# A top-k attention and SwiGLU kernel: one more block by halves, and a different FFN share in the early units

## The chip, the cores and the metric

The kernel runs on one core of one Trainium2 chip. The core has five engines that work side by side, each through its own list of instructions in order: TensorE (matmul, "PE" in the profile; its weight loads are listed apart as "PEld"), VectorE ("DVE"), ScalarE ("ACT"), GpSimd ("POOL") and SyncE ("SP", which issues most DMAs here). The metric is the device time of one execution in microseconds. Lower is better.

## The reference, cut to what matters

The inputs are q, k and v of shape (8, 8, 576, 64): 8 batches, 8 heads, 576 positions, head size 64. Three weight matrices follow for the feed-forward network (FFN).

```python
scores = scale * np.matmul(q, k.transpose(0, 1, 3, 2))
kth = np.partition(scores, -top_k, axis=-1)[..., -top_k:-top_k + 1]     # top_k = 32
scores = np.where(scores >= kth, scores, -1000000000.0)
scores = scores - np.max(scores, axis=-1, keepdims=True)
attn = np.exp(scores)
attn = attn / (np.sum(attn, axis=-1, keepdims=True) + 1e-09)
x = np.matmul(attn, v)                 # then transposed and reshaped to (4608, 512)
g = x @ w_gate                         # 512 -> 1536
silu = g * (1.0 / (1.0 + np.exp(-g)))
out = (silu * (x @ w_val)) @ w_out     # 1536 -> 512
```

All is float32.

## The kernel before, in words

**Units.** Attention is cut into 160 units. A unit is a pair of heads of one batch and a tile of 128 query rows. A batch has 20 units: four full query tiles (576 = 4 x 128 + 64) of four head pairs each, and four units for the last 64 rows. These last units handle one 128-row tile of two half-height heads, so they cost VectorE about half ("short" units below; units 16 to 19, 36 to 39, 56 to 59 and so on). `AHEAD` is 8 * NHP = 32, where NHP = 4 is the number of head pairs.

**What a unit does.** `scores` (lines 288 to 331) multiplies q and k on TensorE and ScalarE copies the result to SBUF as `sc`. `select` (333) finds the 32 largest scores of each row on VectorE: four rounds of MAX8, with a MATCH_REPLACE8 between rounds that writes into the tile `e`. `weigh` (367) turns scores into exponentials on ScalarE, `normalize` (387) divides by their sum (reciprocal on VectorE, one head's multiply on ScalarE and the other's on GpSimd). `turn` (403) transposes the weights on TensorE into a PSUM tile `etps`, and ScalarE copies them to `et`. `values` (423) multiplies by v on TensorE, and ScalarE copies the result into `xT` (465), the input of the FFN. `prep` (257) transposes q and k of a head pair once per batch.

**The FFN.** The 4608 tokens form 18 blocks of 256. For each block, gate and value products (line 604, 256 columns wide) are followed by ScalarE and GpSimd work for the SwiGLU, and then by an output product built from seven quarters (line 670). The first `HALVED` blocks take their gate and value products in two halves of 128 tokens each (`feed_half`, line 502, products in line 517), so that the first half can start before the second half's tokens exist. The first block also has a plain output product (line 569), since the output weights are only combined for the seven quarters later.

**The order of the work.** The main loop (line 870) writes the instructions of all engines unit by unit. In unit n TensorE gets the scores of units ahead, the values of units n-4 and n-3 (even n only), the transposes of unit n-2, prep of a unit ahead, and in between pieces of the FFN. `piece` (777) issues one small piece and returns its cost: 1 for a gate or value step, 0.75 for half a quarter, 0 where no work is ready because tokens are missing. How many pieces a unit gets is set by `share` (813): an allowance of `beside` for a full unit (half of it for a short one) minus a cost for the attention work of that unit, and not less than `least`. What a unit does not use is kept as `credit`, but never more than one piece above the next share. The last four units and the end take all that is left.

Every engine keeps the written order (lines 940 to 953), so a wait of one instruction holds all that follows on its engine. The pools that matter here: `sc` and `e` have three buffers, the PSUM pool `ps_t` (scores, values, transposes, prep) has five, `ps_f` (FFN) three.

Of the kernel before, what the change touches and what calls it, by code (L numbers as in the profile page):

```python
# [25 lines left out]
def kernel(  # L26
# [43 lines left out]
    NHP = H // 2  # L70
# [2 lines left out]
    MS = MC // 2  # L73
    MQ = MC // 2
    NBLK = B * S // BLK
    HALVED = 3
    AHEAD = 8 * NHP
    scale = 1.0 / float(D) ** 0.5
    assert D == 64 and R == 64 and H * D == DM and DM == 512 and B * S % BLK == 0
# [204 lines left out]
    def n_heads(qt):  # L284

        return 1 if qt == J else 2
# [203 lines left out]

    halves_of = {(kb, t): [] for kb in range(HALVED) for t in range(2)}
    fed, told = [], []

    def tokens(kb, t):

        ends = [0]
        for b in range(B):
            ends += [b * S + min(S, (qt + 1) * P) for qt in range(J + 1)]
        end = min(x for x in ends if x >= kb * BLK + (t + 1) * P)
        return NHP * min(end - kb * BLK, BLK)  # L500
# [86 lines left out]
    def feed(kb):  # L587
# [3 lines left out]

        if kb in range(2, HALVED):
            for t in range(2):
# [27 lines left out]
        def pair(m, t):  # L621

            if kb < HALVED:
                return halves_of[kb, t][m // 4][:, m % 4 : m % 4 + 2, :]
# [4 lines left out]

        for s in range(MS if kb >= HALVED else 0):  # L630
            h = ffn.tile([P, 2, BLK], FP32, tag="h", name="h", bufs=MS + 1)
# [145 lines left out]
    def piece():  # L777
# [13 lines left out]
        while True:  # L791
            if not current:
                if not todo or done.get(todo[0], 0) < tokens(todo[0], int(todo[0] >= HALVED)):
                    return 0
# [18 lines left out]
    def share(n):  # L813


        others = 0.0
        for m, cost in [(m, 0.7) for m in valued(n)] + [(n - TURN, 0.6)]:
            if m >= 0:
                others += cost * (0.5 if units[m][1] == J else 1)
        others += 0.7 * len(scored(n))  # L820
        if units[n + 3][1] == 0:
            others += 0.6

        beside = 5.8 if n < AHEAD else 6.25
        least = 2.0 if n >= 3 * NHP and n % 2 == 0 else 0.0
        return max(least, beside * n_heads(units[n][1]) / 2 - others)

    def scored(n):

        ahead = [n + 1] if n < 2 else [] if n % 2 else [n + 1, n + 2]  # L830
        return [m for m in ahead if m < NU and (units[m][1] < J or m % 2 == 0)]

    def valued(n):

        behind = [] if n % 2 else [n - 4, n - 3]
        return [m for m in behind if 0 <= m < NU]
# [33 lines left out]
    for n in range(NU + 3):  # L870
# [16 lines left out]
        if n >= NU - NHP:  # L887
            credit[0] = 8.0
        else:
            credit[0] = min(credit[0] + share(n), share(n) + 1)  # L890
# [93 lines left out]
```

## Time and profile before

| what | us |
|---|---|
| median of 3 runs | 1713.33 |
| lowest, highest | 1712.2, 1714.15 |
| profiled execution | 1712.03 |
| its span in the profile | 1710.2 |
| TensorE busy | 1647.4 (96%) |
| VectorE busy | 1476.5 (86%) |
| ScalarE busy | 1259.5 (74%) |
| GpSimd busy | 799.0 (47%) |

The page cuts the span into 40 slices of 42.8 us, and each digit is the busy share in tenths. "PEclk" is the clock that the throttle granted to TensorE. In a group or a timeline, a line has the start and duration or the busy time, the engine, the line of the kernel, the operation, what is written and read, and the number of instructions; "<-" behind an idle time names what ended it. A float32 matmul shows as two rows in the trace, so one gate or value product of 256 columns is two rows.

### The profile page before, as it was taken

The page shows a single profiled execution, that of the slowest core. Times are in us where ns is not written, and L with a number is a line of the kernel's source. Part 1 is how long each engine was busy: PE and PEld are TensorE (multiplying, and loading weights), DVE is VectorE, ACT ScalarE, POOL GpSimd, SP SyncE. Part 2 cuts the span into 40 slices and gives each one's busy share as a digit, 9 for nine tenths or more (in the row PEclk, how much of TensorE's full clock was granted, in tenths as well). Part 3 has the DMA queues.
Part 4 walks back from the last instruction along what each step waited for, and adds up shares of the span by engine and source line. Part 5 has one row for each costly group of instructions (what it writes and reads, how often), then busy time and mean ns, then how long its engine had stood idle before and what let it go on. Part 6 is the DMA issues. An engine that isn't in the chain of part 4 may idle for free.

```text
span 1710.2 us, 32128 instructions
## 1 busy us (share of the span) xinstructions
PE 1647.4 (96%) x11600; PEld 1398.2 (82%) x11600; DVE 1476.5 (86%) x3311; ACT 1259.5 (74%) x2901; POOL 799.0 (47%) x914
## 2 busy tenths in 40 slices
PE   5588999999999999999999999999999999999999
PEld 3477698987888887888888888888888888888887
DVE  7999899998989899997999989998999979999400
ACT  7899887877767787768676887777777778676531
POOL 4798545352444425353535334444344433535434
PEclk6699999999999999999999999999999999999999
DMA  7533120003000030001200030000400011000000
GB/s 210 139 112 99 29 72 2 14 1 79 22 13 1 15 86 14 1 8 42 51 14 1 13 74 27 2 13 2 98 1 13 2 44 29 13 2 13 1 13 13
DMA packets 109310, 59.74 MB, mean 35 GB/s; under 512 B 88544, under 2 KB 96992, under 8 KB 109152
## 3 DMA queue, kind: packets, MB, share of 16 engines
q1 hardware_dynamic: 108016, 57.37, 12.9%
q8 instruction: 91, 1.49, 0.4%
q14 instruction: 67, 0.55, 0.1%
q10 hardware_dynamic: 1136, 0.33, 0.1%
HBM read 48.23 MB, written 9.44 MB: 34 GB/s over the span
## 4 chain that ended last, share of the span: by engine, by line
PE 88%; DVE 5%; ACT 4%; DMA 1%; POOL 1%; issue 1%; SPq 0%; POOLq 0%; ACTq 0%
PE f L604 37%; PE x_ps L670 10%; PE av L448 9%; PE s L325 8%; PE y_ps L670 8%; PE etps L412 7%; PE f L517 6%; DVE m L347 2%; DVE e L351 2%; PE kqps L271 1%; PE o_ps L569 1%; PE s L308 1%; ACT e L379 1%; DVE size L124 1%; ACT e L374 0%
## 5 line engine op out<-in xcount | busy, mean ns | idle before, releaser
L347 DVE MAX8 m<-e 128x8 f32<-128x576 f32 x864 | 617.9, 755 | 3.3
L351 DVE MATCH_REPLACE8 e<-m,e 128x576 f32<-128x576 f32 x576 | 425.4, 748 | 0.0
L604 PE MATMUL f<-xT,wg 128*128 128x256 f32 x1440 | 335.9, 382 | 1.3 <-ACT xT L465 1.3
L604 PE MATMUL f<-xT,wv 128*128 128x256 f32 x1440 | 331.4, 380 | 0.0
L604 PEld LDWEIGHTS f<-xT,wg 128*128 128x128 f32 x1440 | 268.9, 190 | 49.0 <-issue 13.1
L604 PEld LDWEIGHTS f<-xT,wv 128*128 128x128 f32 x1440 | 268.2, 190 | 37.5 <-issue 3.8
L640 POOL TENSOR_TENSOR h<-h,half_g 128x512 f32<-128x512 f32 x90 | 114.7, 1275 | 349.2 <-ACT h L639 349.2
L330 ACT ACTIVATE sc<-s 128x288 f32<-128x288 f32 x512 | 170.4, 431 | 105.2 <-PE s L325 104.6
L413 ACT COPY et<-etps 128x512 f32<-128x512 f32 (+1 forms) x448 | 183.6, 486 | 66.0 <-PE etps L412 65.6
L379 ACT ACTIVATE e<-e,bias 128x576 f32<-128x576 f32 x288 | 221.7, 780 | 12.7 <-POOL bias L362 9.7
L374 ACT ACTIVATE e<-sc,m 128x576 f32<-128x576 f32 x288 | 212.3, 792 | 0.6 <-DVE m L347 0.5
L351 DVE MATCH_REPLACE8 e<-m,sc 128x576 f32<-128x576 f32 x288 | 212.6, 748 | 0.0
L412 PE MATMUL etps<-ident,e 128*128 128x128 f32 x1312 | 178.2, 280 | 33.7 <-POOL e L399 15.0
L347 DVE MAX8 m<-sc 128x8 f32<-128x576 f32 x288 | 204.0, 747 | 7.5 <-ACT sc L330 7.5
L412 PEld LDWEIGHTS etps<-ident,e 128*128 128x128 f32 x1312 | 156.2, 144 | 54.7 <-POOL e L399 19.2
L645 POOL TENSOR_TENSOR h<-h,val 128x512 f32<-128x512 f32 x90 | 114.8, 1275 | 155.0 <-ACT val L644 152.4
L325 PE MATMUL s<-kqT 64*128 64x288 f32 x1024 | 169.2, 441 | 13.7 <-ACT sc L330 7.5
L399 POOL TENSOR_TENSOR e<-e,tot 128x576 f32<-128x576 f32 x140 | 161.1, 1154 | 28.5 <-DVE tot L393 28.2
L448 PE MATMUL av<-et,v 128*64 128x128 f32 (+1 forms) x2560 | 158.0, 268 | 0.0
L448 PEld LDWEIGHTS av<-et,v 128*64 128x64 f32 x2560 | 137.7, 140 | 5.9 <-ACT kqT L268 2.7
L325 PEld LDWEIGHTS s<-kqT 64*128 64x128 f32 x1024 | 94.2, 190 | 58.3 <-issue 18.4
L397 ACT ACTIVATE e<-e,tot 128x576 f32<-128x576 f32 x148 | 119.1, 805 | 21.7 <-DVE tot L393 21.6
(86 smaller groups left out, 2249.1 us busy)
## 6 DMA issues: line engine op xcount, KB each, us to landing
v<-in_v_dram SPq DMA_DIRECT2D x32, 256.0 KB, 3.3
kq_in<-in_k_dram SPq DMA_DIRECT2D x63, 128.0 KB, 2.8
kq_in<-in_q_dram SPq DMA_DIRECT2D x63, 128.0 KB, 2.9
w<-in_moe_w_gate_dram SPq DMA_DIRECT2D x12, 512.0 KB, 3.8
w<-in_moe_w_val_dram SPq DMA_DIRECT2D x12, 512.0 KB, 3.8
w<-in_moe_w_out_dram SPq DMA_DIRECT2D x12, 512.0 KB, 3.5
out_dram<-o SPq DMA_DIRECT2D x38, 128.0 KB, 2.4
out_dram<-o SPq DMA_DIRECT2D x16, 256.0 KB, 2.5
```

The costliest lines, as they stand in the source:

```text
L325: nc.tensor.matmul(ps[:, 0:half], slab[d, q0 : q0 + P], slab[d, k0 : k0 + half])
L330: nc.scalar.mul(sc[:, i * half : (i + 1) * half], ps[:, 0:half], scale)
L347: nc.vector.max(m[:, t, 8 * r : 8 * r + 8], cur[:, hs])
L351: nc.vector.match_replace(e[:, hs], m[:, t, 8 * r : 8 * r + 8], cur[:, from_[t]], LOWEST)
L374: nc.scalar.activation(e[:, hs], sc[:, at], AF.Prelu, bias=m[:, t, TOP_K - 1 : TOP_K], scale=-1.0, alpha=SMALL,)
L379: nc.scalar.activation(e[:, hs], e[:, hs], AF.Exp, bias=bias[:, t : t + 1], scale=-1.0 / SMALL, accum_out=tot[:, t : t + 1],)
L399: nc.gpsimd.tensor_tensor(e[:, hs], e[:, hs], tot[:, t : t + 1].to_broadcast([P, S]), ALU.mult)
L412: nc.tensor.transpose(ps[:, c * P : (c + 1) * P], e[:, k0 : k0 + P], ident[:])
L413: nc.scalar.copy(et[:, c0 : c0 + cn, :], ps[:, 0 : cn * P].rearrange("p (c j) -> p c j", c=cn),)
L448: nc.tensor.matmul(av[d, i, 0:ql], weights_, moving, start=c == (0 if last else J), stop=c == (J if last else J - 1),)
L604: nc.tensor.matmul(ps[:, i, :], w[:, kc, m * P : (m + 1) * P], x[:, kc, :], start=(kc == 0), stop=(kc == KC - 1),)
L670: nc.tensor.matmul(ps, lhsT, T[i][m], start=m == 0, stop=m == MQ - 1)
```

## The change

Three numbers are changed. `HALVED` goes from 3 to 4, so that block 3, the fourth, takes its gate and value products in halves of 128 tokens, as the first three do. `beside` is 5.2 in place of 5.8 for units 16 to 27 (the 17th to the 28th). `least`, the two pieces that every even unit got at the least from unit 12 on, now applies from unit 32 on.

```diff
-    HALVED = 3
+    HALVED = 4
...
-        beside = 5.8 if n < AHEAD else 6.25
-        least = 2.0 if n >= 3 * NHP and n % 2 == 0 else 0.0
+        beside = 5.2 if 4 * NHP <= n < 7 * NHP else 5.8 if n < AHEAD else 6.25
+        least = 2.0 if n >= AHEAD and n % 2 == 0 else 0.0
         return max(least, beside * n_heads(units[n][1]) / 2 - others)
```

## The prediction

> **What bounds the kernel now.** I read the page's busy shares and slices first, then the chain, then stretches cut at unit borders, then single waits. A unit begins where VectorE runs its first MAX8 on that unit's scores. Units are numbered from 0 as in the code, so "the 33rd unit" is unit 32.
>
> ```profile
> PE 1647.4 (96%) x11600; PEld 1398.2 (82%) x11600; DVE 1476.5 (86%) x3311; ACT 1259.5 (74%) x2901; POOL 799.0 (47%) x914
> ...
> PE   5588999999999999999999999999999999999999
> ...
> PEclk6699999999999999999999999999999999999999
> ...
> PE 88%; DVE 5%; ACT 4%; DMA 1%; POOL 1%; issue 1%; SPq 0%; POOLq 0%; ACTq 0%
> ```
>
> TensorE is short of work only in the first four slices (170 us); after that it carries the end. A microsecond is won after that only by removing a TensorE wait or TensorE work. The stretches show where waits are left: units 16 to 27, 28 to 35, 36 to 37, 38 to 64, 65 to 66.
>
> ```profile
> 193.32:302.76 109.44, 108.04 (x947) 94.37 (x946) 99.76 (x214) 85.38 (x207) 50.41 (x59) 1.00 0.15 37
> 302.76:386.74 83.98, 83.95 (x741) 76.27 (x741) 78.79 (x176) 64.80 (x151) 37.07 (x45) 1.00 0.02 8
> 386.74:400.03 13.29, 11.14 (x128) 9.07 (x128) 11.31 (x26) 10.98 (x28) 5.20 (x7) 1.00 0.25 57
> 400.03:665.15 265.12, 265.12 (x1833) 224.71 (x1830) 243.12 (x555) 199.38 (x465) 111.77 (x136) 1.00 0.13 32
> 665.15:685.06 19.91, 17.59 (x124) 14.39 (x123) 19.84 (x47) 16.75 (x39) 5.79 (x7) 1.00 0.07 27
> ```
>
> After each span come TensorE, weight loads, VectorE, ScalarE and GpSimd, then the granted clock. TensorE is full in 28 to 35 and 38 to 64 and idle 1.4, 2.1 and 2.3 us in the other three. In units 16 to 27 VectorE, not TensorE, has the slack: 9.7 us. What it waits for there (total, times, longest):
>
> ```profile
> DVE e L351 <- PE etps L412: 8.3, 4, 2.7
> ```
>
> A MATCH_REPLACE8 may not overwrite the tile e until the transposes three units back have read it. TensorE has been given too much there and reaches them late.
>
> Units 36, 37 and 65 are dry. Following the plan's credit through the code, these units issue no FFN piece: block 2's output is finished, and block 3 (or 5) waits for tokens. TensorE runs up to VectorE and stands:
>
> ```profile
> 392.76 1.27 PE L412 MATMUL etps<-ident,e 128*128 128x128 f32 x9 [0.38 <-ACT xT L465]
> 395.77 1.20 PE L412 MATMUL etps<-ident,e 128*128 128x128 f32 x9 [1.75 <-ACT e L397]
> ```
> ```profile
> 670.92 0.92 PE L325 MATMUL s<-kqT 64*128 64x288 f32 x4 [0.99 <-ACT et L413]
> ...
> 677.73 2.64 PE L604 MATMUL f<-xT,wg 128*128 128x256 f32 x11 [1.32 <-ACT xT L465]
> ```
>
> Busy time hides part of a wait, as ends of matmuls are modelled. I count from start to start against the usual pace of the same rows (40 rows of av 2.33 us, 8 of s 1.17, 9 of etps 0.98). From 386 to 400 us the excess is 0.3 + 0.45 + 2.1 + 0.2 = **3.0 us**, from 665 to 680 us 1.4 + 1.7 = **3.1 us**. In units 16 to 27 it is 2.7 us (0.58 at 206.81, 0.76 at 222.22, 0.65 at 223.13, 0.57 at 297.29, 0.16 at 277.33).
>
> **The change, part by part.** The order of instructions gives FFN pieces per unit, in the plan's own cost (a piece is 1; half an output quarter, 6 rows of 216 ns or 1.30 us, is 0.75):
> - units 16 to 19: 2, 2, 2, 2 before; 0, 2, 0, 1 after
> - units 20 to 27: 3, 5, 3, 6, 1.75, 5.25, 2.25, 5.25; after 3, 5, 2, 5, 1, 5, 2, 4.5
> - units 28 to 35: 31.5 in all; after 32.25
> - units 36 to 39: 0, 0, 3, 2; after 1.5, 2.25, 2.25, 2.25
> - units 40 to 64: 98.5 before, 98.25 after
> - unit 65: 0; after 5.25. From unit 66 on both orders are the same.
>
> So nothing is moved beyond about 685 us; the end moves by what TensorE does and waits up to there.
>
> *Block 3 by halves.* 192 rows of 256 columns become 384 rows of 128.
>
> ```profile
> 355.39 3.74 PE L517 MATMUL f<-xT,wg 128*128 128x128 f32 x32
> 358.96 1.95 PE L517 MATMUL f<-xT,wv 128*128 128x128 f32 x16
> ...
> 406.17 1.89 PE L604 MATMUL f<-xT,wv 128*128 128x256 f32 x8
> 407.90 0.60 PE L271 MATMUL kqps<-ident,kq_in 128*128 128x128 f32 x4
> ```
>
> By starts, 32 half rows take 3.57 us and 8 full rows 1.73, so two half pieces take 3.57 against 3.46: 0.11 x 12 = **+1.3 us**. The other engines do the same: six gates and six values of 128x512 either way. The early start of a half brings nothing, as block 3 begins only in unit 40, where both halves' tokens are there. From below the edit is 0 (if a weight load covers it), from above 2.8 us, by busy time (71.4 + 70.6 us for 1152 half rows, 667.3 us for 2880 full ones); I take the paces, nearest to a full TensorE.
>
> *Smaller share and no least share, units 16 to 27.* 9 leave in the plan's cost: 3 pieces at 1.79 us and 8 half quarters at 1.30, 15.8 us of TensorE work. VectorE gives back at most the 8.3 us of that row, so TensorE must either use up its lag behind VectorE (2.9 us at unit 28: 305.66 against 302.76) and run ahead, or wait. I walked both engines by the rows above. From 194.34 us unit 16's values and scores and the transposes of unit 14 end near 198.9, in time for e, so the 2.7 us wait in unit 17 goes and unit 18 begins at 204.9 instead of 207.5. Now TensorE, with no piece to run, is late next for three things: in unit 18 the transposes need the bank that the xT copy frees, about 209.1 against 207.9 (1.1 us); in unit 19 they need ScalarE's multiply, queued behind three copies of prep (0.9 us); in unit 20 scores need the bank of the etps copy, queued behind weigh (1.2 + 0.7 us). Units 20 to 27 have 6.9 pieces a pair on the mean: 6.6 us of attention (8 + 8 rows of s, 40 of av, 18 of etps) and 12.2 of FFN against VectorE's two 9.69. A lag of 2 us that prep leaves at unit 21 carries them to unit 28, where the xT copy is late by 0.9. In all about 5.0 us of waits in place of 2.7: **+2.3 us**. Queued behind those transposes are prep and the scores of the unit after next, but VectorE has its scores a unit ahead, so it does not stop. Ends: from below -2.7, if no wait stays; from above +4.5, if of the 15.8 us only the 8.3 come back and no lag is used (7.2 us of waits). I take the walk, between them.
>
> *Refilled units.* In 36 and 37 two and three half quarters stand where TensorE waited, and lag is 2 us at unit 36, so ScalarE's multiply is there first: **-3.0 us**. In 65 seven half quarters (9.1 us) run; unit 66's xT copy then comes during the first two row groups: **-3.1 us**. Ends for each: nothing won (the lag is lower than I think and the same wait comes back) and the whole.
>
> SP: the first output's store moves behind two sets of key and query loads. A load follows the prep two units earlier, some 10 us ahead of its use; four issues took 4.1 us (207.87 to 211.9) and landing takes 2.8 (page, median). GpSimd is idle 54% of units 16 to 27. Both at nothing; with that cover gone a prep comes up to 3 us late.
>
> **Sum:** 1.3 + 2.3 - 3.0 - 3.1 = **-2.5 us** on a profiled execution of 1712.03 us (span 1710.2, 1.8 around it). The median of the runs is 1.3 above that execution: 1713.33 - 2.5 = **1710.8 us**. A measurement of this kernel tells about 0.2% (3.4 us) from no change, and -2.5 is inside.
>
> The row for the clock: TensorE stood from 106.9 to 110.83 us, and then:
>
> ```profile
> 111.16:114.57 3.41, 3.41 (x18) 0.50 0.00 0
> 114.57:118.00 3.43, 1.16 (x11) 1.00 0.68 191
> 118.00:121.40 3.40, 3.18 (x16) 0.50 0.31 120
> ...
> 81.00:88.00 7.00, 4.48 (x39) 1.00 0.30 76
> ```
>
> A wait of 3.8 us was followed by 3.4 us at half clock, and so was the second row with its 2.3 us idle; one wait of 2.5 us in the last row was not. My longest new wait is 1.2 us, so I count nothing.
> The Trainium skill, "TensorE: Matmul & The Clock Gate", Part 1, says one idle window of about 3.4 us puts the array back to half rate, and advises against gaps of about 3 us; that speaks against units with no pieces. By it the sum stays while waits stay under 3 us, and 1.7 us are lost for each longer one; the 2.3 us above show that less can do.
>
> **Rivals.**
> - *TensorE has more lag to use than I think.* Waits in 16 to 28 stay at the old 2.7 or vanish: 1.3 - 6.1 = -4.8, **1708.5 us**, and 1705.8 at the lowest. For it: 8.3 us of VectorE waiting there, which says TensorE is late in four units. Against it: nothing to run in 16 and 18.
> - *Starvation in units 18 to 20, slower.* The three waits there sit one behind another on ScalarE. If they merge to a gap of 2.3 us or more, the waits double (+4.2) and two windows at half clock (3.4 us lost) follow: -2.5 + 7.6 = +5.1, **1718.4 us**; without the clock, 1715.0. It decides from there. For it: ScalarE is busy 78% of that stretch and has one queue. Against it: its FFN copies leave with the pieces.
> - *The refill does not help.* TensorE, given work in 36, 37 and 65, still waits as before: 1.3 + 2.3 = +3.6, **1716.9 us**. Against it: the waits shown come only where pieces were zero.
>
> **How the numbers follow.** Forecast (within 0.2%) 0.46; more lag 0.38; starvation 0.10; no refill 0.06. The last two are slower. The range 1706.6 to 1715.6 leaves out the far part of the first rival and the clock case. The forecast's own range is 1709.9 to 1713.3.
>
> **What would show it.** In the profile after: L517 with 1536 rows and L604 with 2688; no TensorE wait over 0.5 us between units 35 and 67; new waits of etps on xT and e and of s on et, 3 to 4 us together, within 200 to 220 us; VectorE's wait on etps in units 16 to 27 near zero; clock 1.00 after 139 us; unit 28 begins some 8.5 us sooner, unit 67 some 2.5 us. I am wrong if a gap there passes 2.3 us, or if 36, 37 or 65 still wait.

## The result, and the profile after

The changed kernel takes 1716.3 us (19 runs, 1714.21 to 1718.62), the kernel before 1713.31 (19 runs, 1712.06 to 1714.91). The ratio is 1.0018, with a 95% interval of 1.0012 to 1.0025: **3.0 us slower**, where 2.5 us less was forecast. The time lies 0.7 us above the top of the range. The profiled execution took 1716.19 us (span 1714.4).

The page of the changed kernel, busy shares:

```profile
PE 1650.4 (96%) x11792; PEld 1408.6 (82%) x11792; DVE 1476.4 (86%) x3311; ACT 1259.8 (73%) x2901; POOL 799.0 (47%) x914
```

At this grain hardly anything can be told from before, save 192 more matmul rows. The stretches cut at the same units (16 to 27, 28 to 35, 36 to 37, 38 to 64, 65 to 66; span, then TensorE, weight loads, VectorE, ScalarE and GpSimd busy, then the clock) tell more:

```profile
193.46:294.14 100.68, 98.23 (x883) 84.87 (x881) 99.50 (x215) 83.12 (x203) 41.89 (x47) 0.98 0.17 41
294.14:379.88 85.74, 82.61 (x737) 75.87 (x736) 78.65 (x177) 65.64 (x153) 34.90 (x40) 0.98 0.02 8
379.88:394.86 14.98, 14.98 (x121) 12.73 (x120) 11.10 (x26) 9.62 (x24) 9.68 (x14) 1.00 0.02 5
394.86:663.89 269.03, 268.69 (x2061) 233.75 (x2060) 243.05 (x555) 201.39 (x472) 112.85 (x136) 1.00 0.14 34
663.89:684.32 20.43, 20.43 (x134) 17.24 (x133) 19.92 (x47) 13.65 (x33) 8.89 (x12) 1.00 0.07 27
```

The holes are filled: TensorE has no idle time left in units 36 to 37 and 65 to 66, where it had 2.1 and 2.3 us. In units 16 to 27 VectorE no longer waits (99.50 of 100.68 us busy), and unit 28 begins 8.6 us sooner. The new loss is in the second row: 3.1 us of idle TensorE in units 28 to 35, which were full before, and a mean clock of 0.98 in the first two rows. The timeline around unit 29 (start, duration, engine, line, operation) shows that wait:

```profile
303.03 0.73 POOL L657 TENSOR_TENSOR p<-p 128x256 f32<-128x256 f32 x1 [0.91 <-ACT p L704]
303.84 0.73 POOL L657 TENSOR_TENSOR o<-o,p 128x256 f32<-128x256 f32 x1
...
304.53 1.28 POOL L657 TENSOR_TENSOR p<-p,p 128x512 f32<-128x512 f32 x1
...
305.29 0.60 PE L412 MATMUL etps<-ident,e 128*128 128x128 f32 x4
305.76 2.10 POOL L718 TENSOR_TENSOR h<-h,xT 128x256 f32<-128x256 f32 x3
...
307.81 1.15 POOL L399 TENSOR_TENSOR e<-e,tot 128x576 f32<-128x576 f32 x1
...
309.02 1.07 PE L412 MATMUL etps<-ident,e 128*128 128x128 f32 x5 [3.13 <-POOL e L399]
```

GpSimd multiplies the second head of unit 27 by its reciprocal (line 399), and TensorE needs that head for its transposes in unit 29. VectorE had the reciprocal ready at 303.92. But GpSimd's queue first has three sums and three differences of block 1's output (lines 657 and 718), so the multiply starts at 307.81. TensorE stands for 3.1 us, and the clock is then halved. It was halved once before, after a wait of 1.08 us in unit 19. The granted clock is the figure after the busy time:

```profile
213.77:217.18 3.41, 2.33 (x22) 1.00 0.70 175
217.18:220.59 3.41, 3.41 (x44) 0.50 0.80 198
...
305.90:309.02 3.12, 0.00 (x1) 1.00 0.00 0
309.02:312.44 3.42, 3.42 (x12) 0.55 0.02 5
```
```profile
215.00 1.89 PE L325 MATMUL s<-kqT 64*128 64x288 f32 x8 [1.08 <-ACT et L413]
...
218.90 2.06 PE L325 MATMUL s<-kqT 64*128 64x288 f32 x8
```

Counted as in the prediction, by the pace of the rows from start to start, the losses over 0.2 us from unit 16 to unit 29 sum to 10.8 us, in place of 2.7:

| where, in the trace after | us lost |
|---|---|
| waits at the places that the prediction named in units 18 to 20 (0.42, 0.41, 1.20, 0.65) | 2.7 |
| half clock from 217.18 us on (0.76, 0.82) | 1.6 |
| waits in units 24 to 26 (0.55, 0.56, 0.41) | 1.5 |
| unit 29: the wait for GpSimd 3.61, and half clock after it 1.42 | 5.0 |

The 0.76 us is easily missed: the 40 value rows of a short unit take 2.07 us there (216.82 to 218.90), but 1.31 us at full clock (224.95 to 226.27 in the kernel before). So the term is +8.1 us where +2.3 was forecast. With +1.4 for the half rows, +0.8 for a wait at unit 60, and -6.1 for the holes, +4.2 comes out. The same group of block 5's rows begins at 703.38 us instead of 699.25, which is +4.0 after the 0.14 us by which unit 16 begins later. These are the two profiled executions, 1712.03 and 1716.19 us; the medians lie 3.0 us apart.

### The profile page after: what moved, and what is told of

It reads as the page before. It is cut to its first block, busy times and chain, and to the rows that moved or that the text cites. A ratio compares the mean times of both kernels' runs of the same rounds, so it can differ in the third digit from the quotient of the medians.

```text
span 1714.4 us, 32508 instructions
## 1 busy us (share of the span) xinstructions
PE 1650.4 (96%) x11792; PEld 1408.6 (82%) x11792; DVE 1476.4 (86%) x3311; ACT 1259.8 (73%) x2901; POOL 799.0 (47%) x914
## 4 chain that ended last, share of the span: by engine, by line
PE 84%; DVE 8%; ACT 4%; POOL 1%; DMA 1%; issue 1%; SPq 1%; ACTq 0%; POOLq 0%
PE f L604 34%; PE x_ps L670 10%; PE av L448 9%; PE s L325 8%; PE y_ps L670 7%; PE etps L412 7%; PE f L517 6%; DVE m L347 4%; DVE e L351 4%; PE kqps L271 1%; PE o_ps L569 1%; PE s L308 1%; ACT e L379 1%; DVE size L124 1%; ACT et L413 1%
## 5 line engine op out<-in xcount | busy, mean ns | idle before, releaser
L604 PE MATMUL f<-xT,wg 128*128 128x256 f32 x1344 | 313.0, 382 | 0.0
L604 PE MATMUL f<-xT,wv 128*128 128x256 f32 x1344 | 308.5, 380 | 0.0
L604 PEld LDWEIGHTS f<-xT,wg 128*128 128x128 f32 x1344 | 251.0, 190 | 44.6 <-issue 13.1
L604 PEld LDWEIGHTS f<-xT,wv 128*128 128x128 f32 x1344 | 250.7, 190 | 33.5 <-issue 2.3
L640 POOL TENSOR_TENSOR h<-h,half_g 128x512 f32<-128x512 f32 x84 | 107.0, 1274 | 346.9 <-ACT h L639 346.9
L325 PE MATMUL s<-kqT 64*128 64x288 f32 x1024 | 169.3, 441 | 14.5 <-ACT sc L330 7.9
L645 POOL TENSOR_TENSOR h<-h,val 128x512 f32<-128x512 f32 x84 | 107.1, 1275 | 139.8 <-ACT val L644 137.4
```

The lines of the kernel that those rows point to most:

```text
L325: nc.tensor.matmul(ps[:, 0:half], slab[d, q0 : q0 + P], slab[d, k0 : k0 + half])
L604: nc.tensor.matmul(ps[:, i, :], w[:, kc, m * P : (m + 1) * P], x[:, kc, :], start=(kc == 0), stop=(kc == KC - 1),)
```

## The experiments

Two theories were set against each other. A: the loss is new TensorE waits and half clock in units 16 to 29, above all the one behind GpSimd, while the halves are a plain extra of 1.3 us. B: the halves are the loss and the shares are even. A third, C, came up later: the empty short units are the loss. Each group of runs has the kernel before beside it (medians 1713.6 to 1714.0), and a gain over it is against the median of the same group. Differences between changed versions are taken between their medians; the kernel before moved by up to 0.6 us from group to group (1713.31 to 1713.95).

**e1: the shares without the halves.**

```diff
-    HALVED = 4
+    HALVED = 3
```

> The changed kernel with its halves edit undone (HALVED back to 3); shares and least as changed. The plan gives every unit the same pieces as in the changed kernel, only block 3's rows are 256 wide again. Theory A (the loss sits in new TensorE waits and two stretches of half clock in units 16 to 29; the halves edit is a plain extra of about 1.3 us): 1715.0 us, 1.3 below the changed kernel, still above before. Rival B (the halves edit is the loss and the shares are even): 1713 us or less, 3 or more below the changed kernel.

Measured: 1714.76 us, ratio to before 1.0009 (1.0000 to 1.0018). Against the changed kernel it is 1.5 us shorter, as A has it. The halves bring nothing in this plan and cost what their rows cost; without them the shares still don't win. Its trace has the wait of 3.1 us on GpSimd and both stretches of half clock.

**e2: the halves alone.** The kernel before with the one line `HALVED = 4`.

> The kernel before with only the halves edit (HALVED 4). Units 36 and 37 now get 2 pieces each, because half of block 3 is there earlier; units 64 and 65 are both dry instead of 65 alone. Theory A: the 3.0 us of waits at units 36 and 37 go, 1.3 us of rows come, and the waits at 65 and 66 grow by 0 to 3: 1711.6 to 1714.6 us. Rival B: 1716 us.

Measured: 1719.6 us, ratio 1.0035 (1.0023 to 1.0048), slower than both theories said. The wait at 392 to 397 us is gone, as expected. But the pieces that run in units 36 to 39 are now missing later. TensorE's four longest waits in units 57 to 69 (total, times, longest):

```profile
PE etps L412 <- ACT e L397: 1.8, 1, 1.8
PE s L325 <- ACT sc L330: 1.6, 1, 1.6
PE s L325 <- ACT et L413: 1.4, 1, 1.4
PE f L604 <- ACT xT L465: 1.4, 1, 1.4
```

Counted by the pace of the rows, units 64 to 66 lose 8.5 us where before they lost 3.1, and block 3's output quarters lose 2.1 us at 460 to 484 us. With -3.0 for the hole filled and +1.3 for the rows that makes +5.8 us, which is what was measured (1719.6 against 1713.8). Tokens come at VectorE's pace. A block begun sooner leaves a longer hole at the next stop, and here the longer hole cost more than the one it filled. I had put 0 to 3 us on that.

**e3: the multiply of unit 27 on ScalarE.** One instruction changes its engine:

```diff
-            if t == 0 and n >= 3 * NHP:
+            if (t == 0 or n == 27) and n >= 3 * NHP:
                 nc.scalar.mul(e[:, hs], e[:, hs], tot[:, t : t + 1])
```

> The changed kernel, with the second head's multiply of unit 27 alone moved from GpSimd's queue to ScalarE, so that it doesn't stand behind the sums of block 1's output. Theory A: the 3.1 us wait of the transposes in unit 29 and the half clock after it (1.4 us) go: 1716.3 - 4.5 = 1711.8 us, and 4 us less spread between runs is left. Rival B, or if another wait takes its place: 1716 us, no change.

Measured: **1711.41 us**, ratio 0.9984 (0.9975 to 0.9993), 4.9 us below the changed kernel. This one instruction's place in a queue was worth more than the whole loss. The same place in e3's timeline:

```profile
305.91 1.44 ACT L397 ACTIVATE e<-e,tot 128x576 f32<-128x576 f32 x2 [1.00 <-DVE tot L393]
...
306.47 1.28 POOL L657 TENSOR_TENSOR p<-p,p 128x512 f32<-128x512 f32 x1
307.24 1.15 PE L412 MATMUL etps<-ident,e 128*128 128x128 f32 x9
307.71 2.11 POOL L718 TENSOR_TENSOR h<-h,xT 128x256 f32<-128x256 f32 x3
```

ScalarE does both multiplies after the reciprocal, the nine transposes run in one go, and GpSimd's sums go on beside them. The half clock at this place is gone too; the one from 217 us on (219 here) stays. From the start of unit 16 to the first gate row of block 10, e3's trace takes 841.5 us, that of the changed kernel 846.5 and that of the kernel before 842.5. So the 5 us are won in this stretch, and a half clock of 3.41 us near 1647 us, which e3's trace lacks and the other two have, is no part of them. The part of the expectation on the spread did not hold: the runs go from 1708.96 to 1712.71.

**e6: e1 and e3 together.** `HALVED = 3` and the line of e3.

> Both: the changed shares without the halves edit, and unit 27's second multiply on ScalarE. Theory A: the two gains add, 1716.3 - 1.3 - 4.5 = 1710.5 us, below before (1713.3). Rival B: as e1.

Measured: 1710.25 us, ratio 0.9979 (0.9970 to 0.9988). The gains add (1.2 below e3), and this version is faster than both kernels. Its trace has the same waits of 1.20 and 0.65 us (215.8 to 219.0 us) as e3's, but no half clock after them. The time that this saves it waits for later: 2.1 us at 257 to 265 us, where e3 waits 0.6.

**e7: only the edit of `least`, and e8: only that of `beside`.** Both with `HALVED = 3`.

```diff
-        least = 2.0 if n >= 3 * NHP and n % 2 == 0 else 0.0
+        least = 2.0 if n >= AHEAD and n % 2 == 0 else 0.0
```
```diff
-        beside = 5.8 if n < AHEAD else 6.25
+        beside = 5.2 if 4 * NHP <= n < 7 * NHP else 5.8 if n < AHEAD else 6.25
```

> The kernel before with only the edit of least (from unit 32 instead of 12; beside and HALVED as before). Units 16 and 18 get no piece, units 36 and 37 get 2.25 and 0.75, unit 65 stays dry. Theory A (each edit of the shares costs its own new waits and wins the holes it fills; the GpSimd wait of unit 29 comes only with the lower beside, which leaves TensorE no lag): waits of 3.9 us in units 18 to 20 in place of 2.0, the 3.0 us at 36 and 37 gone, 3.1 us at 65 stay: 1713.6 + 1.9 - 3.0 = 1712.5 us, 1711 to 1714. Rival C (empty short units are the loss): 1716 us or more.

> The kernel before with only beside 5.2 in units 16 to 27 (least and HALVED as before). Units 16 to 18 keep 2 pieces, 36 and 37 get 1.5 and 2.25, 65 gets 0.75. Theory A: no new wait in units 18 to 20, about 1 us of new waits on xT in 24 to 28, 3.0 us at 36 and 37 gone, most of the 3.1 us at 65 stay: 1711.5 us; if the GpSimd wait comes too, 4 more. Rival C: 1711 us without any GpSimd wait.

Measured: e7 1710.54 us, ratio 0.9982 (0.9973 to 0.9991); e8 1710.51, ratio 0.9979 (0.9970 to 0.9988). Each half of the share edit alone wins 3.3 us, e7 0.5 us more than the range of A allowed. C falls: with units 16 and 18 empty, e7 is faster, and its clock does not drop. Neither trace has a wait of transposes on GpSimd. Put together (e1) the two edits are 0.9 us slower than before: each fills units 36 and 37, and the second adds only unit 65. What the sum of both brings is the wait in unit 29. In e1 TensorE is ready for the second head of unit 27 at 305.8 us, and the multiply, behind the six sums and differences, ends at 308.8. In e7 and e8 TensorE comes later, and the output block falls otherwise, with one sum ahead of the multiply: it ends at 311.3 and 313.4, and the transposes begin at 315.8 and 314.9. So lag and the place of the sums both count; no run separates them.

**e9: the control.** The kernel before with the line of e3.

> A control: the kernel before, with unit 27's second multiply on ScalarE as in e3. There TensorE is 2.9 us behind VectorE at unit 28 and doesn't wait for that multiply. Theory A: 1713.6 us, no change (within 1). If the move by itself were a gain (GpSimd freed), 1711 or less.

Measured: 1713.61 us, ratio 0.9999 (0.9991 to 1.0008). No change: in the trace of before that multiply ends at 315.4 us and its transposes begin at 320.3. Moving the multiply is worth something only where TensorE arrives before it.

**e10: one piece more in the empty units.** e6, with

```diff
-        least = 2.0 if n >= AHEAD and n % 2 == 0 else 0.0
+        least = (2.0 if n >= AHEAD else 1.0 if n >= 4 * NHP else 0.0) if n % 2 == 0 else 0.0
```

and the multiplies of units 24 to 31 on ScalarE.

> e6 with at least one piece in the even units 16 to 31 (so units 16 and 18 get one each) and the second multiply on ScalarE in units 24 to 31. Theory A: the piece in unit 18 stands where TensorE waits for the xT copy, and the half clock after unit 20 goes: 1 to 2 us below e6 (1710.3), 1708.8 us. If those waits only move behind the piece: 1710.3 us.

Measured: 1723.35 us, ratio 1.0056 (1.0042 to 1.0069), a clear miss by 14.5 us. Its trace has no half clock near unit 20, but neither has e6's, so that gain was not there to be won. Two more pieces in units 16 and 18 shift later output blocks against the units, and three of them now meet a multiply that TensorE waits for. By the pace of the rows the three waits cost 6.4 us and the half clock after the second 1.7; the rest of the loss is not assigned, as the run also moves seven more multiplies than e6. One of the three in e10's timeline:

```profile
579.11 2.11 POOL L718 TENSOR_TENSOR h<-h,xT 128x256 f32<-128x256 f32 x3
579.41 0.60 PE L412 MATMUL etps<-ident,e 128*128 128x128 f32 x4
581.17 1.16 POOL L399 TENSOR_TENSOR e<-e,tot 128x576 f32<-128x576 f32 x1
...
582.38 0.77 PE L412 MATMUL etps<-ident,e 128*128 128x128 f32 x5 [2.37 <-POOL e L399]
```

It is the order of unit 29 in the changed kernel again; three sums of line 657 stand ahead of these lines here too.

**e11: e10 with those three multiplies moved.** `n in (45, 53, 63)` is added to the condition of e3's line.

> e10, which came out at 1723.4 us, with the second multiply of units 45, 53 and 63 on ScalarE too. Its trace has three waits of transposes on GpSimd's multiply (1.9 us at 491.9, 2.6 us at 579.4, 1.9 us at 678.4), each behind three sums L657 and three L718 of an output block, and 1.7 us more at half clock after the second. Theory A (these collisions are the loss, as at unit 29 of the changed kernel): 1723.4 - 8 = 1715.3 us. If something else made e10 slow: 1721 us or more.

Measured: 1716.39 us, ratio to before 1.0016 (1.0007 to 1.0025), 7.0 us below e10 where 8 were expected. The three waits are gone from the trace. What stays slow in it are waits of block outputs for GpSimd's own sums (1.63 us at 304, 1.87 at 375 to 383) and of scores on ScalarE.

**e12 and e13: a smaller share from unit 32.** e7, with `6.05 if n < 66 else 6.25` (e12) and `6.1 if n < 66 else 6.25` (e13) in place of 6.25.

> e7 (1710.5 us: the kernel before with least from unit 32) with beside 6.05 in place of 6.25 in units 32 to 65, so that unit 65 keeps 5.25 pieces. Theory A: the 3.1 us at units 65 and 66 go, at no price where TensorE has lag: 1707.4 us; up to 4 us back for each collision of transposes with an output block's sums on GpSimd.

> As e12, with beside 6.1: unit 65 gets 3.75 pieces. Theory A: 1708 us, as e12, but the output blocks fall on other units, so collisions with GpSimd can differ by 2 to 4 us each.

Measured: e12 1713.73 us, ratio 0.9996 (0.9988 to 1.0005); e13 1713.76, ratio 1.0001 (0.9993 to 1.0010). Both miss A's 1707.4 and 1708 us; e12 exceeds the 4 us that A allowed for one collision. The hole at unit 65 is filled in both, and the gain is eaten: e12 has a wait of 2.6 us on GpSimd's multiply at 575 us and 2.0 us for GpSimd's sums and differences at 553 to 562; e13 has two such waits on the multiply, 1.9 us at 573 and 3.2 us at 667 us, and 1.6 us of prep waiting for ScalarE's copies at 595 to 597.

**e14: e13 with those two multiplies moved** (units 53 and 63, same line).

> e13 (1713.8 us) with the second multiply of units 53 and 63 on ScalarE, the two behind which its transposes waited on GpSimd (1.9 and 3.2 us). Theory A: 1713.8 - 5.1 = 1708.7 us, the shortest of all. If the wait passes to the bias that GpSimd still works out behind the sums (ScalarE's exponentials, then VectorE): 1711 us or more.

Measured: 1710.17 us, ratio 0.9978 (0.9969 to 0.9987), 3.6 us below e13; 5.1 were expected. Both waits are gone from the trace, a wait of 0.64 us at 675 us has come, and the 1.6 us of prep stay. This is level with e6, e7 and e8 within the measurement; all four are faster than both kernels.

## Why the prediction was wrong

- *The holes: -3.0 and -3.1 us.* Right. Neither wait is in the trace after.
- *The halves: +1.3 us, with nothing gained.* Right: 1.5 us (changed kernel to e1) and 1.2 us (e3 to e6), and the rows by busy time stay below the upper end of 2.8.
- *Units 16 to 20.* Right in place, and in part in size: 1.1, 0.9 and 1.9 us were worked out, 0.42, 0.41 and 1.85 measured. VectorE's wait on etps vanished, and unit 28 began 8.6 us sooner (8.5 forecast).
- *"In all about 5.0 us of waits in place of 2.7: +2.3 us."* This is the term that failed; it was 10.8 and +8.1, beyond its own upper end of +4.5. That end was set too low: with 15.8 us of work gone and only 8.3 us given back, waits grow by 7.5 us, from 2.7 to 10.2, where the prediction took 7.2 us for the whole. What the term held, waits on TensorE's other suppliers, came to 4.2 us, though 1.5 of them lay in units 24 to 26, where it had none, in place of 0.9 at unit 28. What it left out was GpSimd. I walked TensorE, VectorE and ScalarE, but not GpSimd, which the prediction set aside as "idle 54% of units 16 to 27. Both at nothing". The transposes of unit 27 stand in unit 29, just past the stretch whose idle share I used, and what counted was not how busy GpSimd was but what stood ahead of one instruction: 4.8 us of output sums and differences. By the walk's own numbers the lag of 2 us was used up at unit 28, so it should have been asked what makes the second head ready as well as the first. e3 shows that this wait, with the clock after it, was 4.9 us; without it, the kernel is at 1711.4 us, 0.6 above the forecast. That it comes so near is partly luck, as the clock, the sizes of the waits and the wait at unit 60 were not as worked out.
- *"My longest new wait is 1.2 us, so I count nothing" for the clock.* Wrong: after the 1.08 us wait at 215 us the clock was halved from 217.18 to 220.59 us, and once more after the 3.1 us wait. The second cost 1.4 us. The first took 1.6 us where it stood, but cost little in the end: e6, which did not have it, waits 1.5 us more than e3 soon after (2.1 us against 0.6). This rests on one trace of each.
- *The rivals.* "Starvation" had the right sign, for the wrong queue: it put the merged wait on ScalarE in units 18 to 20. A half clock did come there, but after a wait of 1.08 us, not after the merged one of 2.3 us that the rival asked for. (Its doubled waits, +4.2, stand against 3.9 us of waits that the walk names there.) GpSimd was no rival at all.

Why the 19 runs differ is open, as only one was profiled. Their times lie in three clusters (1714.2 to 1714.8, 1715.5 to 1716.3, 1717.3 to 1718.6 us), 1.5 us apart. None, one or two clock drops would be a guess, but the profiled execution, which had both, lies in the middle cluster and not in the last.

## What to carry to other kernels

Lag of a bound engine behind its suppliers is a buffer: when work is taken from it, go through each queue that feeds its next instructions, the idle ones too, and ask what stands ahead of them in program order. Pieces of one plan share one supply, so a hole filled here is paid for at the next stop (e2), and small edits that each win can lose together (e7, e8, e1). A stretch at half clock can cost little where the engine would have had to wait soon after (e6 against e3). Where a few instructions' phase decides, move the one instruction that is waited for (e3, e14) before retuning the shares.

## What the runs showed of the hardware

The clock was halved after less of a gap than I took from the trace of before. The window from 213.77 to 217.18 us had TensorE busy for 2.33 of 3.41 us, with one wait of 1.08 us among transposes and narrow score and value rows, and the next 3.41 us ran at 0.50. Counted by the pace of the rows, that window held about 1.5 us of work. All drops after 100 us in these traces last 3.41 or 6.83 us, but for the last one of each trace, which stops with it. Within a trace they begin on one grid: in the changed kernel 217.18, 309.34 and 1647.36 us lie 27 and 392 steps of 3.413 us apart.

The same waits do not always bring a drop. In e6 they fall across a border of the grid, and the window with most of the wait (216.28 to 219.70 us) held about 1.9 us of row work; no drop followed. In e7 (waits of 1.38 and 0.65 us by the pace of the rows) the window from 215.30 to 218.71 us held about 1.9 us too, and none followed, though by the profile it was busy for 2.15 us, less than the window of the drop. The work between row starts tells these cases apart and the busy time does not. It gives no threshold: in e2 the window from 681.37 to 684.78 us held about 1.5 us and no drop followed. What the throttle counts is not shown here.

The Trainium skill, "TensorE: Matmul & The Clock Gate", Part 1, puts the return to half rate after one idle window of about 3.4 us. The window lengths here agree with it, and so does the drop at 309.34 us, whose window was idle for 3.1 of 3.4 us; the drop after a window that was 68% busy by the profile does not, and the measurement decides.
